# Output stage of a fused attention and gated-MLP kernel: order of the two products that share each PSUM bank

## The chip, the cores and the metric

The kernel runs on one core of one Trainium2 chip. The metric is device microseconds of one execution. Before the change it is 206.86 us, the median of 3 runs (206.8 to 207.03). Beside these there is one execution under the profiler, from which all rows below come.

## The reference

The input x has 2048 tokens of 512 features. It is normalised (xn), and three things are added: x itself, a local attention, and a gated MLP.

```python
xn = _layernorm(x)
# attention: 32 heads of 16; each token looks at 8 keys, 2 tokens apart, itself first
qkv = xn @ wqkv
o = softmax(q . k[s - 2*w]) . v[s - 2*w]      # w = 0..7, positions under 0 masked
A = o.reshape(S, 512) @ wo
# gated MLP: 688 + 688 features
z = gelu(xn @ w_in)
z1, z2 = z[:, :688], layernorm(z[:, 688:])
g = w_sp @ z2 + b_sp                          # 2048 x 2048, mixes tokens
B = (z1 * g) @ w_out
out = x + A + B
```

## The kernel before, in words

**Stages.** The first part (up to about 73 us) normalises x, makes z2, q, k and v, and forms the attention weights. The long middle part runs over 16 row tiles j of 128 tokens. `mix(j)` (line 488) multiplies the mixing matrix by z2 (32 matmuls, line 492), `z1_tile(j)` (line 500) makes the gate (8 matmuls, line 504), and `gate_out(j)` (line 512) multiplies the two on VectorE (line 514) and puts the product, transposed by a DMA, into `uT` (line 515). `uT` holds the gated features on partitions, in 6 chunks of 128, by 2048 tokens. Meanwhile VectorE forms the attention's outputs `op` in a generator `av_ops` (line 550), from which `vector_work(us)` (line 575) takes pieces; the last pieces are an addition at line 563, one at line 565 and the closing one at line 567, which writes `op` for the last quarter of the tokens. The order on every engine is the order in which the program issues: there is no scheduler.

**Layout of `op`.** Its 128 partitions are 4 bands of 32 heads; a band k holds 256 tokens of a half (half 0 is tokens 0 to 1023, half 1 the rest). On the free axis stand the 16 features of a head, and 512 columns: four blocks of 128 columns, which the program calls jj = 0 to 3. jj 0 and 1 belong to half 0, jj 2 and 3 to half 1. So a group jj is four token tiles, one for each band k, and the tile number is i = 8 (jj // 2) + 2 k + jj % 2.

**Output stage (lines 627 to 659).** A token tile's output is one PSUM bank, 128 tokens by 512 features in fp32, and is made of two products:

- the *attention's part* A(jj), line 635: 14 of the 16 head features (`DHA`), 56 matmuls for a group. Each uses 32 rows of the array (`tile_position=(32 * k, 0)`), and the four bands run beside each other into four banks. "A set" below is four such matmuls, one for each band.
- the *gated part* B(jj, k), line 646: 6 matmuls with all 128 rows for a token tile. The free rows of the last chunk of `uT` hold the two head features that A leaves out; `op_rest(hb, queue)` (line 543) copies them there by 8 DMAs for a half, for half 0 on SP's queue at j = 13, for half 1 on ScalarE's queue after group 0.

The eight banks are two pools of four, `ps_o[0]` for even jj and `ps_o[1]` for odd jj. The order on TensorE is A(0), A(1), B(0, 0..3), B(1, 0..3), then A(2), A(3), B(2, 0..3), B(3, 0..3). A opens a bank and B closes it. After each B(jj, k), VectorE adds the token tile of x (`xrs`, two buffers of four tiles, loaded by `load_xr`, line 585) to the bank and writes `ot` (line 650, four buffers), and SP stores `ot` (line 651). The bank of jj + 2 is the bank of jj, so A(2) waits for the evictions of group 0 and A(3) for those of group 1. The very last tile (3, 3) goes another way: its attention part is taken out early, with x added, into `rest` (line 654), and `last_tile` (line 614) makes B in two halves of 256 columns in banks of its own, with two shorter evictions (line 623) and two stores (line 624). `load_xr(2)` and `load_xr(3)` stand on SP's queue behind the stores of groups 0 and 1.

Of the kernel before, what the change touches and what calls it, by code (L numbers as in the profile page):

```python
# [7 lines left out]
BF16 = mybir.dt.bfloat16  # L8
F32 = mybir.dt.float32
ACT = mybir.ActivationFunctionType  # L10
ALU = mybir.AluOpType
PSUM = bass.MemoryType.PSUM

P = 128
S = 2048
D = 512
# [4 lines left out]
DHA = 14  # L21
# [5 lines left out]
NG = 4  # L27
# [4 lines left out]
MCH = 6  # L32
# [13 lines left out]
def kernel(  # L46
# [16 lines left out]
    V = nc.vector  # L63
    A = nc.scalar
    G = nc.gpsimd
    PE = nc.tensor
    SP = nc.sync

    x2 = A_x.rearrange("b s d -> (b s) d")
    out2 = out.rearrange("b s d -> (b s) d")  # L70
# [414 lines left out]
    uT = late.tile([P, MCH, S], BF16, name="uT")  # L485
# [48 lines left out]
    pwp = ctx.enter_context(tc.tile_pool(name="pwp", bufs=3, reuse_waits="tile", **right))  # L534
    xrp = ctx.enter_context(tc.tile_pool(name="xrp", bufs=2, reuse_waits="tile", **right))
    smp = ctx.enter_context(tc.tile_pool(name="smp", bufs=1, reuse_waits="tile", **right))
    otp = ctx.enter_context(tc.tile_pool(name="otp", bufs=4, reuse_waits="tile", **right))
    op = late2.tile([P, DH, NB * TG], BF16, name="op")
    wo_r = late2.tile([P, DHA, D], BF16, name="wo_r")
    wout = late2.tile([P, MCH, D], BF16, name="wout")  # L540
    G.memset(wout[32:64, MCH - 1, :], 0.0)

    def op_rest(hb, q):

        for k in range(NG):
            for e in range(2):
                q.dma_start(uT[64 + 32 * e:96 + 32 * e, MCH - 1, hb * SB + k * TG:hb * SB + (k + 1) * TG],
                             op[32 * k:32 * k + 32, DHA + e, hb * TG:(hb + 1) * TG])
# [26 lines left out]
    def vector_work(us):  # L575
        while us > 0:
            t = next(work, None)
            if t is None:
                return
            us -= t  # L580

    x_g = x2.rearrange("(b k q p) d -> b q p k d", b=NB, k=NG, q=2)
    xrs = []

    def load_xr(jj):
        xr = xrp.tile([P, NG, D], BF16, name="xr")
        SP.dma_start(xr[:], x_g[jj // 2, jj % 2])
        xrs.append(xr)

    vector_work(2.0)  # L590
    for j in range(3, NT):
        z1_tile(j, mix(j))
        if j == 3:
            pair_b.close()
            ps_o = [ctx.enter_context(tc.tile_pool(name="ps_o0", bufs=4, space=PSUM, reuse_waits="tile"))]
# [8 lines left out]
        if 6 <= j < 10:  # L604
            k = j - 6
# [8 lines left out]
    def last_tile(i, rest):  # L614

        ot = otp.tile([P, D], BF16, name="ot")
        for h in range(2):
            ns = slice(h * D // 2, (h + 1) * D // 2)
            po = ps_o[0].tile([P, D], F32, name="po")
            for m in range(MCH):  # L620
                PE.matmul(po[:, ns], uT[:, m, i * P:(i + 1) * P], wout[:, m, ns],  # L621
                          start=(m == 0), stop=(m == MCH - 1))
            V.tensor_tensor(ot[:, ns], po[:, ns], rest[:, ns], ALU.add)
            SP.dma_start(out2[i * P:(i + 1) * P, ns], ot[:, ns])


    ps_o.append(ctx.enter_context(tc.tile_pool(name="ps_o1", bufs=4, space=PSUM, side="right", reuse_waits="tile")))
    for pair in range(2):
        pos = {}
        for jj in (2 * pair, 2 * pair + 1):  # L630
            for k in range(NG):
                pos[jj, k] = ps_o[jj % 2].tile([P, D], F32, name="po")
            for d in range(DHA):
                for k in range(NG):
                    PE.matmul(pos[jj, k][:], op[32 * k:32 * k + 32, d, jj * P:(jj + 1) * P],  # L635
                              wo_r[32 * k:32 * k + 32, d, :],
                              start=(d == 0), stop=((jj, k, d) == (3, NG - 1, DHA - 1)), tile_position=(32 * k, 0))
        for jj in (2 * pair, 2 * pair + 1):
            hb, q = jj // 2, jj % 2
            for k in range(NG):  # L640
                i = 8 * hb + 2 * k + q
                if (jj, k) == (3, NG - 1):
                    last_tile(i, rest)
                    continue
                for m in range(MCH):
                    PE.matmul(pos[jj, k][:], uT[:, m, i * P:(i + 1) * P], wout[:, m, :],  # L646
                              start=False, stop=(m == MCH - 1))
                vector_work(2.0)
                ot = otp.tile([P, D], BF16, name="ot")
                V.tensor_tensor(ot[:], pos[jj, k][:], xrs[jj][:, k, :], ALU.add)  # L650
                SP.dma_start(out2[i * P:(i + 1) * P, :], ot[:])
                if (jj, k) == (2, 0):
                    rest = pwp.tile([P, D], F32, name="rest", tag="pw")
                    V.tensor_tensor(rest[:], pos[3, NG - 1][:], xrs[3][:, NG - 1, :], ALU.add)
            if jj == 0:
                vector_work(1e9)
                op_rest(1, A)
            if jj + 2 < 4:
                load_xr(jj + 2)


# [1 line left out]
_INS = ['A_x', 'A_wqkv', 'A_wo', 'B_x', 'B_w_in', 'B_w_sp', 'B_b_sp', 'B_w_out']  # L663
_OUTS = [((1, 2048, 512), 'bfloat16')]
# [25 lines left out]
```

## Time and profile before

| what | value |
|---|---|
| median of the runs | 206.86 us |
| the profiled execution, its own time | 206.6 us |
| its span, first to last instruction | 204.9 us |
| TensorE (PE) busy, share of the span | 200.3 us, 98% |
| VectorE (DVE) busy | 166.1 us, 81% |
| ScalarE (ACT) busy | 93.5 us, 46% |
| granted TensorE clock, mean | 0.999 |
| first matmul of the output stage | 168.64 us after the span's start |
| last eviction (line 623) begins | 202.01 us after the span's start |

How to read it: the page of a profile gives busy times, the span in 40 slices, the chain of work that ended last (followed back from the last instruction), and groups of instructions by source line. PE are matmuls and PEld the loads of the stationary operand, which overlap them. SPq and ACTq are the queues from which DMAs are issued. Matmuls are pipelined: one of 512 columns takes some 379 ns from start to end, while the next starts sooner, so a busy PE may still start its matmuls later than it could. Their ends are modelled and a few records are missing.

### The profile page before, as it was taken

The numbers are of one execution on the slowest core, as the hardware profiler recorded it, in microseconds if no ns is written. First come the engines' busy times: TensorE is split into PE (matmuls) and PEld (weight loads), VectorE is DVE, ScalarE is ACT, GpSimd is POOL, SyncE is SP. The second block draws the span as 40 slices with busy tenths as digits, with TensorE's granted clock in tenths as the row PEclk, the third lists the DMA queues.
The fourth block names the chain that finished last, engine by engine and source line by source line (L and its number), as shares of the span: only waits on it lengthen the run. The fifth ranks groups of instructions, "written<-read, shape, count | busy, mean of one in ns | idle before, by whom it ended". The sixth has DMA issues, their size and how long they took to land.

```text
span 204.9 us, 4056 instructions
## 1 busy us (share of the span) xinstructions
PE 200.3 (98%) x1660; PEld 120.7 (59%) x1666; DVE 166.1 (81%) x192; ACT 93.5 (46%) x145; POOL 16.1 (8%) x82
## 2 busy tenths in 40 slices
PE   7999999999999999999999999999999999999994
PEld 7755554555566666656666666666666664444442
DVE  4899949659299599989999999999999985582353
ACT  3868897676879996335733331213333320000000
POOL 5045630000000000100000000000000000000000
PEclk9999999999999999999999999999999999999999
DMA  6973846999000004718766799999565225047323
GB/s 170 363 223 78 198 95 154 213 212 117 4 3 0 3 0 44 154 32 163 122 129 141 179 210 187 218 175 187 114 145 140 56 48 80 26 99 218 110 99 97
DMA packets 67395, 25.64 MB, mean 125 GB/s; under 512 B 57152, under 2 KB 67248, under 8 KB 67248
## 3 DMA queue, kind: packets, MB, share of 16 engines
q1 hardware_dynamic: 66960, 25.24, 57.6%
q8 instruction: 13, 0.21, 0.4%
q10 hardware_dynamic: 416, 0.14, 0.3%
q14 instruction: 6, 0.05, 0.1%
HBM read 9.79 MB, written 2.10 MB: 58 GB/s over the span
## 4 chain that ended last, share of the span: by engine, by line
PE 96%; DVE 1%; DMA 1%; issue 0%
PE pg L492 36%; PE pq L260 10%; PE po L646 9%; PE pzb L229 9%; PE pz L504 9%; PE pv L285 7%; PE po L635 6%; PE pl L310 4%; PE pq L272 3%; DMA xq<-in_A_x_dram 1%; PE po L621 1%; PE pt L212 1%; DVE stats L185 1%; PE idle L100 0%; DVE xn L190 0%
## 5 line engine op out<-in xcount | busy, mean ns | idle before, releaser
L492 PE MATMUL pg<-z,wspT 128*128 128x344 bf16 x512 | 77.3, 309 | 0.0
L492 PEld LDWEIGHTS <-wspT 128*128 128x128 bf16 x512 | 50.0, 98 | 24.9 <-issue 0.4
L301 DVE TENSOR_TENSOR pr<-qk 128x8192 bf16<-128x8192 bf16 x8 | 35.0, 4420 | 7.4 <-PE pl L310 7.4
L495 ACT ACTIVATE gs<-pg,b_col 128x688 bf16<-128x688 f32 x16 | 13.3, 833 | 52.9 <-PE pg L492 52.9
L558 DVE TENSOR_TENSOR pw<-vp,a_sb 128x4096 bf16<-128x4096 bf16 x16 | 36.1, 2284 | 0.0
L650 DVE TENSOR_TENSOR ot<-po,xr 128x512 bf16<-128x512 f32 x15 | 10.2, 689 | 15.2 <-PE po L646 14.9
L260 PE MATMUL pq<-xnT,wqk 128*128 128x512 bf16 x93 | 21.4, 379 | 0.2
L504 PE MATMUL pz<-w_z,xnT 128*128 128x344 bf16 x128 | 21.3, 309 | 0.0
L229 PE MATMUL pzb<-w_z,xnT 128*128 128x344 bf16 x128 | 20.1, 309 | 0.0
L646 PE MATMUL po<-wout,uT 128*128 128x512 bf16 x88 | 19.3, 379 | 0.3 <-issue 0.3
L563 DVE TENSOR_TENSOR pw<-pw 128x4096 bf16<-128x4096 bf16 x8 | 18.3, 2288 | 0.1
L229 PEld LDWEIGHTS <-xnT 128*128 128x128 bf16 x128 | 12.3, 98 | 7.0 <-issue 0.4
L504 PEld LDWEIGHTS <-xnT 128*128 128x128 bf16 x128 | 12.4, 98 | 6.5 <-issue 0.4
L260 PEld LDWEIGHTS <-wqk 128*128 128x128 bf16 x96 | 9.3, 98 | 10.9 <-issue 0.4
L646 PEld LDWEIGHTS <-uT 128*128 128x128 bf16 x90 | 8.6, 98 | 11.0 <-issue 0.8
L263 ACT CAST qk<-pq 128x1024 bf16<-128x1024 f32 x12 | 12.1, 1012 | 5.4 <-PE pq L260 5.4
L285 PE MATMUL pv<-xnT,wv 128*32 128x512 bf16 x256 | 14.6, 380 | 0.0
L509 ACT ACTIVATE z<-pz 128x688 bf16<-128x688 f32 x16 | 11.9, 743 | 5.6 <-PE pz L504 5.2
L238 ACT ACTIVATE junk<-z 128x688 bf16<-128x688 bf16 x16 | 12.4, 778 | 0.2
L635 PE MATMUL po<-wo_r,op 32*128 32x512 bf16 x224 | 12.4, 375 | 0.0
L234 ACT ACTIVATE z<-pzb 128x688 bf16<-128x688 f32 x16 | 11.8, 735 | 1.4 <-PE pzb L229 1.4
L285 PEld LDWEIGHTS <-wv 128*32 128x32 bf16 x256 | 9.4, 139 | 4.6 <-issue 0.3
(81 smaller groups left out, 169.2 us busy)
## 6 DMA issues: line engine op xcount, KB each, us to landing
xr<-in_A_x_dram SPq DMA_DIRECT2D x4, 512.0 KB, 4.1
out_dram<-ot SPq DMA_DIRECT2D x15, 128.0 KB, 1.8
wo_r<-in_A_wo_dram SPq DMA_DIRECT2D x4, 448.0 KB, 4.8
w_z<-in_B_w_in_dram SPq DMA_DIRECT2D x2, 688.0 KB, 4.9
xq<-in_A_x_dram SPq DMA_DIRECT2D x2, 512.0 KB, 7.0
wqk<-in_A_wqkv_dram SPq DMA_DIRECT2D x2, 512.0 KB, 7.0
wout<-in_B_w_out_dram SPq DMA_DIRECT2D x1, 640.0 KB, 5.2
a_sb<-in_A_x_dram SPq DMA_DIRECT2D x1, 512.0 KB, 9.1
```

The costliest lines, as they stand in the source:

```text
L229: PE.matmul(pz[:, hh, 0:FHALF], xnT[:, kc, i * P:(i + 1) * P], w_z2[:, kc, hh * FHALF:(hh + 1) * FHALF], start=(kc == 0), stop=(kc == C - 1))
L238: A.activation(junk[:], z2[:, i, :], ACT.Square, accum_out=zsq[:, i:i + 1])
L260: PE.matmul(pq[:, s, :], wqk[:, kc, s, c * P:(c + 1) * P], xnT[:, kc, tsl], start=(kc == 0), stop=(kc == C - 1))
L285: PE.matmul(pv[32 * k:32 * k + 32, dd, :].rearrange("p (b t) -> p b t", b=NB), wv_v[:, kc, 2 * d2 + dd, :], xnT_g[:, kc, :, k, :], start=( ...
L301: V.tensor_tensor(pr[:], qk[hb][:, 0, :, HALO:HALO + SB].unsqueeze(1).broadcast_to([P, 2, C, SB]), shifted(qk[hb][:, 1, :, off:off + SB]), ...
L492: PE.matmul(pg[:, hh, 0:FHALF], wsps[j][:, k, :], z2[:, k, hh * FHALF:(hh + 1) * FHALF], start=(k == 0), stop=(k == NT - 1))
L495: A.activation(gs[:], pg[:, :, 0:FHALF], ACT.Identity, bias=b_col[:, j:j + 1])
L504: PE.matmul(pz[:, hh, 0:FHALF], xnT[:, kc, j * P:(j + 1) * P], w_z1[:, kc, hh * FHALF:(hh + 1) * FHALF], start=(kc == 0), stop=(kc == C - 1))
L558: V.tensor_tensor(pw[:], shifted(vp[:, :, hb, off:off + P]), a_sb[:, 2 * p:2 * p + 2, osl].unsqueeze(2).broadcast_to([P, 2, DH, P]), ALU.mult)
L563: V.tensor_tensor(pws[p - 1][:], pws[p - 1][:], pw[:], ALU.add)
L635: PE.matmul(pos[jj, k][:], op[32 * k:32 * k + 32, d, jj * P:(jj + 1) * P], wo_r[32 * k:32 * k + 32, d, :], start=(d == 0), stop=((jj, k, d ...
L646: PE.matmul(pos[jj, k][:], uT[:, m, i * P:(i + 1) * P], wout[:, m, :], start=False, stop=(m == MCH - 1))
```

## The change

The output stage is written in another order. The other functions, the data and the number of matmuls, evictions and DMAs are the same. On TensorE the order becomes B(0, 0..3), B(1, 0..3), which open all eight banks; then A(0), A(1), which close them; then A(2) and A(3), which open them anew; then B(2, 0..3), B(3, 0..3), which close them. The remaining attention work of VectorE and `op_rest(1, A)` are issued ahead of the first eviction. The four evictions and stores of group 0 follow A(0), those of group 1 follow A(1), with `load_xr(2)` and `load_xr(3)` behind them. `rest` is taken ahead of the eviction of (2, 0) and no longer behind it. In `last_tile` only the notation differs.

```diff
+    def out_b(jj, k, first):
+        i = tokens_of(jj, k)
+        if first:
+            pos[jj, k] = ps_o[jj % 2].tile([P, D], F32, name="po")
+        for m in range(MCH):
+            PE.matmul(pos[jj, k][:], uT[:, m, i * P:(i + 1) * P], wout[:, m, :],
+                      start=first and m == 0, stop=not first and m == MCH - 1)
...
+    def out_a(jj, first):
+        for k in range(NG):
+            if first:
+                pos[jj, k] = ps_o[jj % 2].tile([P, D], F32, name="po")
+        for d in range(DHA):
             for k in range(NG):
-                pos[jj, k] = ps_o[jj % 2].tile([P, D], F32, name="po")
-            for d in range(DHA):
-                for k in range(NG):
-                    PE.matmul(pos[jj, k][:], op[32 * k:32 * k + 32, d, jj * P:(jj + 1) * P],
-                              wo_r[32 * k:32 * k + 32, d, :],
-                              start=(d == 0), stop=((jj, k, d) == (3, NG - 1, DHA - 1)), tile_position=(32 * k, 0))
+                PE.matmul(pos[jj, k][:], op[32 * k:32 * k + 32, d, jj * P:(jj + 1) * P],
+                          wo_r[32 * k:32 * k + 32, d, :], start=first and d == 0,
+                          stop=(not first or (jj, k) == (3, NG - 1)) and d == DHA - 1, tile_position=(32 * k, 0))
...
+    for jj in range(2):
+        for k in range(NG):
+            out_b(jj, k, True)
+    vector_work(1e9)
+    op_rest(1, A)
+    for jj in range(4):
+        out_a(jj, jj > 1)
+        if jj < 2:
             for k in range(NG):
-                i = 8 * hb + 2 * k + q
...
-                vector_work(2.0)
-                ot = otp.tile([P, D], BF16, name="ot")
-                V.tensor_tensor(ot[:], pos[jj, k][:], xrs[jj][:, k, :], ALU.add)
-                SP.dma_start(out2[i * P:(i + 1) * P, :], ot[:])
-                if (jj, k) == (2, 0):
-                    rest = pwp.tile([P, D], F32, name="rest", tag="pw")
-                    V.tensor_tensor(rest[:], pos[3, NG - 1][:], xrs[3][:, NG - 1, :], ALU.add)
-            if jj == 0:
-                vector_work(1e9)
-                op_rest(1, A)
-            if jj + 2 < 4:
-                load_xr(jj + 2)
+                store(jj, k)
+            load_xr(jj + 2)
+    rest = pwp.tile([P, D], F32, name="rest", tag="pw")
+    V.tensor_tensor(rest[:], pos[3, NG - 1][:], xrs[3][:, NG - 1, :], ALU.add)
+    for jj in range(2, 4):
+        for k in range(NG):
+            if (jj, k) == (3, NG - 1):
+                last_tile(tokens_of(jj, k), rest)
+            else:
+                out_b(jj, k, False)
+                store(jj, k)
```

`store(jj, k)` is the eviction and the store of a tile as before (lines 649 to 651).

## The prediction

> **What bounds the kernel.** I read the page first, then the chain of waits in order of time, then the timeline of the output stage from 168 us on.
>
> From the page of before:
>
> ```profile
> PE 200.3 (98%) x1660; PEld 120.7 (59%) x1666; DVE 166.1 (81%) x192; ACT 93.5 (46%) x145; POOL 16.1 (8%) x82
> PEclk9999999999999999999999999999999999999999
> PE 96%; DVE 1%; DMA 1%; issue 0%
> L646 PE MATMUL po<-wout,uT 128*128 128x512 bf16 x88 | 19.3, 379 | 0.3 <-issue 0.3
> L646 PEld LDWEIGHTS <-uT 128*128 128x128 bf16 x90 | 8.6, 98 | 11.0 <-issue 0.8
> ```
>
> TensorE is the bound: 98% busy, 96% of the chain, at full clock all along. The last two lines show that two matmuls of line 646 have no record: 90 weight loads, 88 matmuls. That will matter.
>
> The end of the chain in order of time (start, length, engine, tile, line, count):
>
> ```profile
> 167.54 1.17 PE pz L504 x8
> 168.71 6.16 PE po L635 x112
> 174.87 0.16 issue
> 175.03 10.31 PE po L646 x47
> 185.33 6.15 PE po L635 x112
> 191.49 0.16 issue
> 191.65 9.01 PE po L646 x41
> ```
>
> Nothing but matmuls ends last in the output stage, and the only holes stand where the attention's part (L635) gives way to the gated part (L646). So only fewer holes or a new wait of TensorE can change the time.
>
> The timeline around a hole, and VectorE's part of the same time:
>
> ```profile
> 174.27 0.60 PE L635 MATMUL po<-wo_r,op 32*128 32x512 bf16 x8
> 174.80 0.55 PEld L646 LDWEIGHTS <-uT 128*128 128x128 bf16 x4 [0.42 <-issue]
> 175.03 0.59 PE L646 MATMUL po<-wout,uT 128*128 128x512 bf16 x2 [0.16 <-issue]
> ...
> 176.31 0.69 DVE L650 TENSOR_TENSOR ot<-po,xr 128x512 bf16<-128x512 f32 x1 [4.01 <-PE po L646]
> 176.91 2.28 DVE L565 TENSOR_TENSOR pw<-pw 128x4096 bf16<-128x4096 bf16 x1
> 179.11 0.69 DVE L650 TENSOR_TENSOR ot<-po,xr 128x512 bf16<-128x512 f32 x1
> 179.71 1.22 DVE L567 TENSOR_TENSOR op<-pw 128x2048 bf16<-128x2048 bf16 x1
> 180.85 1.88 DVE L650 TENSOR_TENSOR ot<-po,xr 128x512 bf16<-128x512 f32 x3
> ```
>
> **The step of a matmul.** 47 recorded matmuls take 10.31 us: (10.31 - 0.38) / 46 = 0.216 us from start to start. The attention's part has the same step for a set of four: the 28 sets of a pair of groups take 6.22 us in the timeline, (6.22 - 0.38) / 27 = 0.216.
>
> **What is removed: two changes of array mode.** TensorE changes between 128 rows and 32 rows four times now: gate to A(0), A(1) to B(0), B(1) to A(2), A(3) to B(2). After, the gate is followed by B (both 128 rows), so only B(1) to A(0) and A(3) to B(2) are left. The prices:
>
> - Gate to A: the gate's last matmul starts at 168.40, its step is 0.146 (1.17 / 8), the first of A is due at 168.55 and starts at 168.64: **0.09**.
> - A(1) to B and B to A(2) together: from the first matmul of A(0), 168.64, to that of A(2), 185.27, are 16.63 us. In them lie 28 sets and 48 matmuls, 76 x 0.216 = 16.42. The rest is **0.21** for the two.
> - A(3) to B: from 185.27 to the first matmul of line 621 at 200.50 are 15.23 us for 28 + 42 steps, 15.12: **0.11**.
>
> So each change costs about 0.10 us, 0.41 in all, of which 0.21 stay: **-0.20 us**. This is less than the rows seem to offer. The first B matmul is recorded at 175.03, 0.53 after the last set of A (174.49), which reads as a loss of 0.32; the weight loads sit idle 0.42. But this is where a record is missing: 48 loads stand against 47 matmuls in the stretch, the second load starts at 174.81, and elsewhere a load starts when the matmul ahead of it does. The eviction settles it. It begins at 176.31; other evictions begin 0.42 us after the sixth matmul of their tile starts (the one at 185.37 after the matmul of 184.96). Counted from an unrecorded matmul at 174.81 the sixth starts at 175.89, 0.42 before; counted from 175.03 it starts at 176.11, 0.20 before, which is shorter than the matmul's own 0.38.
>
> **What is moved, on TensorE.** B(0) and B(1) now start at 168.55. They need the gated features of tiles 0 to 7, whose transposes are long done, and the eight copies of half 0, the last of which SP issues at 164.20 and which land 1.8 later, at 166.0; the first use is later than 168.55. The banks of `ps_o[1]` are free when the last gate is evicted (168.80 + 0.74 = 169.54); B(1) gets there at 168.55 + 24 x 0.216 = 173.73. B ends at 168.55 + 48 x 0.216 = 178.92, so A(0) starts at 179.02, A(1) at 182.04, A(2) at 185.07, A(3) at 188.09, and B(2) at 179.02 + 56 x 0.216 + 0.10 = 191.22. Before, it starts at 191.65 - 0.22 = 191.43 (its first matmul is the other one without a record): again 0.21 earlier. From there on the order is the old one, with the same tail: last matmuls, evictions of 0.42, two stores.
>
> **What is moved, on VectorE.** Line 563 ends at 172.29, and lines 565 and 567 follow at once, as nothing of the stores stands between them: 172.3 + 2.2 + 1.2 = 175.8 in place of 180.9. A(2), which reads it, starts at 185.07. The 4.01 us for which VectorE now waits ahead of its first eviction cost nothing, and their going gains nothing. The eight copies of half 1 on ScalarE's queue start at 175.8 and take 5.1 us to issue, as now; the last landed 4.0 later at most, which would be 185, and B(2) asks for them after 191. The covers are 9 and 6 us.
>
> **The added wait: A(2) and A(3) on evictions just before them.** Now there are 6 to 8 us of B between the closing of a bank and its reuse. After, A(0) closes all four banks in its last set, and A(2) wants them one group later, 14 x 0.216 = 3.02 us. Behind a waiting matmul stands all of TensorE. A(0)'s last set starts at 179.02 + 13 x 0.216 = 181.83, the first eviction at +0.42 = 182.25; evictions follow each other at 0.60 (180.85, 181.45, 182.04: three in 1.88 us), and the fourth ends at 182.25 + 1.80 + 0.69 = 184.74, against 185.07: **0.33 us to spare**. Group 1: last set at 184.85, evictions from 185.27, the fourth ends at 187.76 against 188.09: again 0.33. An answer from VectorE to a waiting engine is quick: the store's issue stands at 177.03, 0.03 after the eviction's end at 177.00. So I take nothing for this wait; below nothing it cannot be.
>
> The rule that speaks against this is in the Trainium skill, "TensorEngine Tiling (Array Packing)", section "PSUM Bottleneck": after a fourfold faster TensorE the PSUM copy may become the bottleneck, and both ScalarE and VectorE should empty it. The row says 2.49 us of evictions against 3.02 us of matmuls, so here VectorE alone just holds. "TensorE: Matmul & The Clock Gate", section "The cost: per-tile semaphore tail", adds that the completions of packed tiles which each raise a semaphore are served one after another, 25 + 4.7 x 4 + 26.3 x 4 = 149 ns for four tiles, an estimate by its formula; no row of before has four such closings. It would eat less than half of the spare time and leave the sum as it is.
>
> **The buffers of the stores.** `ot` has four. The evictions of group 1 start 3.02 us after those of group 0 and need their stores landed. Store k is issued at 182.97 + 0.60 k, the eviction that reuses its buffer wants to start at 185.27 + 0.60 k: it waits where landing takes over 2.3 us. From the list of DMA issues, narrowed to the stores issued at 177.03, 179.83 and 183.53, and to the three from 197 to 201 (the last column is us to landing):
>
> ```profile
> out_dram<-ot SPq DMA_DIRECT2D x1, 128.0 KB, 1.7
> out_dram<-ot SPq DMA_DIRECT2D x1, 128.0 KB, 3.0
> out_dram<-ot SPq DMA_DIRECT2D x1, 128.0 KB, 3.7
> out_dram<-ot SPq DMA_DIRECT2D x3, 128.0 KB, 1.7
> ```
>
> The median of all 15 is 1.8. The one at 3.7, and another at 184.02 with the same time, were issued right behind the 512 KB load `xr` (182.58). After, the four stores of group 0 stand ahead of that load on SP and those of group 1 behind it, where nobody soon waits for them. So I take 1.8 and no wait, with 1.7 and 3.7 as ends.
>
> **The rest.** `load_xr(3)` is issued near 188.2 and lands 4.1 later, at 192.3. `rest` now stands ahead of (2, 0) on VectorE and waits for it until 192.3, so the eviction of (2, 0) starts near 192.9 and not at its 192.7; then 0.6 to 0.7 of VectorE face 1.30 of TensorE per tile, and this is caught up within a tile. Nothing. Evictions beside four-band matmuls: the one at 185.37 lies beside A(2) now, takes 0.69 as others do, and the sets beside it keep their step. Nothing.
>
> **Sum.** -0.20 us on an execution of 206.6 (204.9 of span and 1.7 around it) gives 206.4. The median of the runs is 0.26 above that execution, so I forecast **206.66**. About 0.2%, or 0.41 us, is what a measurement of this kernel can tell from no change; the gain is half of that.
>
> **Rivals.**
>
> 1. *The holes are as large as recorded.* Then a change from A to B costs 0.32, the one removed at the gate 0.09, and -0.41 or somewhat more follows: 206.4. For it stand the recorded starts, against it the missing record and the eviction at 176.31. 15%.
> 2. *A store lands late, by a little.* With landing time L the fourth eviction of group 1 ends at 184.77 + L + 0.69, and A(3) stalls for L - 2.63. At 3.0 (one store in the trace) the stall is 0.37, the net +0.17: 207.03, still no change to measure. 12%.
> 3. *VectorE's release of the banks becomes the bound (slower).* The same place, A(3) behind the evictions of group 1 behind the stores of group 0, at a landing of 3.7 as beside a 512 KB load: stall 1.07, net +0.87, 207.7. It decides for slower from L = 3.24 on. For it: those two stores; against it: their place behind the load, which these stores don't have. 12%.
>
> That the order isn't the one described is excluded: TensorE's instructions, listed, stand in it, and their number is the old one.
>
> **Chances and range.** Forecast 61% (2 of them spill over to faster and 1 to slower), rivals 15, 12 and 12. Faster by over 0.2%: 0.17. Within: 58 + 12 = 0.70. Slower: 0.13. The range takes in rivals 1 and 2 and the near end of 3: 206.35 to 207.3.
>
> **What would show it.** Right: L639 begins within 0.02 us of 168.55 with no hole, two holes are left, A(0) to A(3) run as 56 sets in 12.1 us, and VectorE's fourth evictions end 0.2 to 0.3 before A(2) and A(3). Wrong: an idle TensorE in front of A(2) or A(3) with an eviction (rival 3: behind a store) as releaser; or a span shorter by 0.4 or more with the same two holes (rival 1).

## The result, and the profile after

The changed kernel takes 207.8 us (median of 17 runs, 206.75 to 209.01), the kernel before in the same sessions 206.8 (17 runs, 206.47 to 207.91): ratio 1.0039, interval 1.0023 to 1.0055. It is slower by some 0.8 to 1.0 us, outside the range of the forecast, and its runs spread wider. The profiled execution took 207.98 us, its span is 206.3.

The first line of the page after hardly tells the difference: TensorE is at 98% as before, and VectorE a point lower.

```profile
PE 201.2 (98%) x1666; PEld 120.9 (59%) x1666; DVE 166.0 (80%) x192; ACT 93.6 (45%) x145; POOL 16.1 (8%) x82
```

The chain of waits in order of time (start, length, what) no longer consists of matmuls alone:

```profile
168.86 10.36 PE po L639 x48
179.22 3.17 PE po L648 x56
182.39 1.89 DVE ot L655 x3
...
184.29 3.30 DMA out_dram<-ot
...
188.33 1.29 DVE ot L655 x2
...
189.66 3.18 PE po L648 x53
192.84 9.17 PE po L639 x42
```

The first row answers to the forecast: the gated part follows the gate without a hole. Then the chain leaves TensorE for evictions of group 0 (L655), a store of theirs (`out_dram<-ot`, 3.30 us) and evictions of group 1, and comes back to TensorE only at 189.66, in A(3).

The timeline of the same stretch:

```profile
179.15 9.68 PE L648 MATMUL po<-wo_r,op 32*128 32x512 bf16 x170
182.38 2.48 DVE L655 TENSOR_TENSOR ot<-po,xr 128x512 bf16<-128x512 f32 x4 [6.35 <-PE po L648]
183.10 3.04 SPq L656 DMA_DIRECT2D out_dram<-ot  x4
...
187.12 2.48 DVE L655 TENSOR_TENSOR ot<-po,xr 128x512 bf16<-128x512 f32 x4 [2.26 <-DMA out_dram<-ot]
...
189.06 0.37 PE L648 MATMUL po<-wo_r,op 32*128 32x512 bf16 x1 [0.23 <-DVE ot L655]
189.66 3.18 PE L648 MATMUL po<-wo_r,op 32*128 32x512 bf16 x53 [0.23 <-DVE ot L655]
```

VectorE has done group 0 at 184.86. The first bank of group 1 is closed and could be emptied near 185.4, but VectorE starts at 187.12, after 2.26 us of idle time that a store ended. Its four evictions then free the banks one by one: the second, third and fourth matmul of A(3), each into a bank of its own, start 0.05 us after an eviction ends. A(3) is due at 179.15 + 42 x 0.216 = 188.22; its fourth matmul starts at 189.66. **Stall: 1.43 us.**

Why the stores are late, from the list of DMAs, each narrowed to a stretch of the trace (183.0 to 183.5, 183.5 to 184.2, 184.2 to 184.85, 184.85 to 186.1). An issue's last column is us to landing; a queue's are packets, MB and share of the 16 engines' time in the stretch:

```profile
out_dram<-ot SPq DMA_DIRECT2D x1, 128.0 KB, 3.8
out_dram<-ot SPq DMA_DIRECT2D x1, 128.0 KB, 3.6
q8 instruction: 1, 0.02, 13.4%
out_dram<-ot SPq DMA_DIRECT2D x1, 128.0 KB, 3.3
out_dram<-ot SPq DMA_DIRECT2D x1, 128.0 KB, 3.0
```

All four land late, and among them begins a transfer of another kind: one packet of 16 KB on an instruction queue. 13.4% of 16 engines over 0.65 us is 1.39 us on one engine. From 185.7 to 186.45 only 9 packets move in the whole core, one after the other, between two stretches at over 300 GB/s. Here is that stretch, and below it a store that had the DMA engines to itself, in the kernel before (177 to 179):

```profile
DMA packets 9, 0.01 MB, mean 11 GB/s; under 512 B 1, under 2 KB 9, under 8 KB 9
DMA packets 144, 0.13 MB, mean 66 GB/s; under 512 B 16, under 2 KB 144, under 8 KB 144
```

A whole store is 144 packets, 16 of them small; a sixteenth of it is 9 packets, one of them small. So the stretch is read as one engine of the sixteen working off its share of the first store, which had waited behind the fetch, while fifteen are done. The count fits, but that it is one engine stays inferred; the records do not name engines.

### The profile page after: what moved, and what is told of

It reads as the page before. It is cut to its first block, busy times and chain, and to the rows that moved or that the text cites. A ratio compares the mean times of both kernels' runs of the same rounds, so it can differ in the third digit from the quotient of the medians.

```text
span 206.3 us, 4066 instructions
## 1 busy us (share of the span) xinstructions
PE 201.2 (98%) x1666; PEld 120.9 (59%) x1666; DVE 166.0 (80%) x192; ACT 93.6 (45%) x145; POOL 16.1 (8%) x82
## 4 chain that ended last, share of the span: by engine, by line
PE 94%; DVE 2%; DMA 2%; ACT 1%; issue 0%; DVEq 0%
PE pg L492 36%; PE pq L260 10%; PE po L639 9%; PE pzb L229 9%; PE pz L504 9%; PE pv L285 7%; PE pl L310 4%; PE pq L272 3%; PE po L648 3%; PE idle L100 2%; DVE ot L655 2%; DMA out_dram<-ot 2%; PE po L621 1%; ACT xnT L214 1%; PE pt L212 0%
## 5 line engine op out<-in xcount | busy, mean ns | idle before, releaser
L639 PE MATMUL po<-wout,uT 128*128 128x512 bf16 x90 | 19.8, 379 | 0.0
L655 DVE TENSOR_TENSOR ot<-po,xr 128x512 bf16<-128x512 f32 x15 | 9.8, 686 | 11.9 <-PE po L648 6.4
L648 PE MATMUL po<-wo_r,op 32*128 32x512 bf16 x224 | 13.2, 374 | 0.5 <-DVE ot L655 0.5
```

## The experiments

**Theories.** F: the instruction fetch holds the stores of group 0 on one DMA engine, the four `ot` buffers pass the delay to VectorE's next evictions, these to the banks, and the banks to A(3). S: four stores in a row are slow by themselves. E: VectorE's evictions of four banks are too slow for one group of matmuls, whatever the stores do. The clean measure is the *stage*: from the start of the last gate matmul (line 504) to the start of the very last matmul (line 621) in the timeline, 33.29 us before and 34.50 after. The start of the kernel spreads by itself, as will be seen.

**e1: seven output buffers.**

```diff
-    otp = ctx.enter_context(tc.tile_pool(name="otp", bufs=4, reuse_waits="tile", **right))
+    otp = ctx.enter_context(tc.tile_pool(name="otp", bufs=7, reuse_waits="tile", **right))
```

> The changed kernel with seven output buffers ot instead of four, so that the evictions of (1,0), (1,1) and (1,2) no longer wait for a store of group 0 and (1,3) alone reuses the first buffer. Theory F (a 16 KB instruction fetch occupies one DMA engine while the four stores of group 0 pass, their landing takes 3.0 to 3.8 us, and the reuse of ot passes this on to VectorE, the banks and A(3)): the stores still land in 3 us or more, but VectorE starts on group 1 near 185.4 and A(3) loses at most 0.1; the median is 0.2 us under the kernel before, ratio 0.999, 1.2 us under the changed kernel. Theory S (four stores in a row are slow by themselves): the same time, it is told apart by the shift of the fetch. Theory E (the evictions of four banks are too slow for a group of 3.02 us, whatever the stores do): no change, 207.8.

Measured: median 206.88 us (11 runs), ratio 1.0000 (0.9991 to 1.0009). The timeline of its profile (the stage begins 0.83 us later here):

```profile
179.98 12.27 PE L648 MATMUL po<-wo_r,op 32*128 32x512 bf16 x224
183.21 2.48 DVE L655 TENSOR_TENSOR ot<-po,xr 128x512 bf16<-128x512 f32 x4 [6.35 <-PE po L648]
...
186.23 2.48 DVE L655 TENSOR_TENSOR ot<-po,xr 128x512 bf16<-128x512 f32 x4 [0.54 <-PE po L648]
```

All 56 sets run in one piece, and VectorE starts on group 1 exactly 3.02 us after group 0, though three of the four stores still land after 3.1, 2.8 and 2.5 us. The stage is 33.08. So theory E is out: evictions alone keep pace. The reuse of `ot` is what passes the delay on. The median was expected 0.2 us under the kernel before and did not show it; this was followed up in e6 and e9.

**e2 and e3: moving the fetch.** 104 more TensorE instructions at the very start, in the changed kernel (e2) and in the kernel before (e3):

```diff
-    spin(26)
+    spin(14)
+    for _ in range(64):
+        PE.matmul(idle[0:32, 0, 0:32], ones[:, 0:32], ones[:, 0:32], start=True, stop=True)
```

> The changed kernel with 52 more matmuls (104 more instructions with their weight loads) among the warm-up matmuls at the very start: 14 large and 64 small ones in place of 26 large ones. TensorE's instructions are fetched every 256, so the fetch at 184.4 should fall 104 instructions, that is 13 sets or 2.8 us, earlier in the output stage, near 181.6 after the same start, and end before the first store's packets. Theory F: the stores of group 0 land in about 1.8 us, no stall at A(3), the time is 0.2 us under the same edit of the kernel before (e3), and 1.2 under the changed kernel but for what the start costs. Theory S: the stores land in 3 us or more with no fetch among them and the time is 1 us over e3.

> The kernel before with the same edit at the start as e2, its control. Both theories: the time of the kernel before, within 0.3 us, plus or minus what the other warm-up does to the start; only the difference to e2 is used.

Measured: e2 206.40 us (11 runs), ratio to the kernel before 0.9987 (0.9977 to 0.9998); e3 206.77, ratio 1.0000 (0.9992 to 1.0009). In e2 the fetch begins 13.55 us after the last gate matmul, where it began 15.83 after in the changed kernel (2.3 us earlier; 2.8 had been expected), and is over before the first store's packets. The four stores of group 0 in e2, in their order:

```profile
out_dram<-ot SPq DMA_DIRECT2D x1, 128.0 KB, 1.8
out_dram<-ot SPq DMA_DIRECT2D x1, 128.0 KB, 1.7
out_dram<-ot SPq DMA_DIRECT2D x1, 128.0 KB, 1.7
out_dram<-ot SPq DMA_DIRECT2D x1, 128.0 KB, 1.8
```

Four stores in a row, 0.6 us apart, each on time: theory S is out. The stage is 33.08 in e2 and 33.29 in e3. The pair also explains the odd store that the prediction had seen, the one at 3.0 us in the kernel before, issued at 179.83. Its stretch of the trace (180.2 to 180.5) holds a fetch:

```profile
q8 instruction: 1, 0.02, 28.9%
```

In e3, where the fetches lie elsewhere, the same store is issued at 179.95 and lands after 1.7 us. In e7 below, again the kernel before with a fetch beside this store, it lands after 3.3.

**e4: eight changes of array mode.** The kernel before with each group's B right behind its A:

```diff
-    for pair in range(2):
-        pos = {}
-        for jj in (2 * pair, 2 * pair + 1):
...
-        for jj in (2 * pair, 2 * pair + 1):
-            hb, q = jj // 2, jj % 2
+    pos = {}
+    for jj in range(4):
+        for k in range(NG):
+            pos[jj, k] = ps_o[jj % 2].tile([P, D], F32, name="po")
...
+        hb, q = jj // 2, jj % 2
+        if jj == 3:
+            rest = pwp.tile([P, D], F32, name="rest", tag="pw")
+            V.tensor_tensor(rest[:], pos[3, NG - 1][:], xrs[3][:, NG - 1, :], ALU.add)
+        for k in range(NG):
```

> The kernel before with the order A(0) B(0) A(1) B(1) A(2) B(2) A(3) B(3): eight changes between 128 and 32 rows in place of four, and no bank that is reused soon after its closing. By the prediction's price of 0.10 us for a change: +0.41 us, ratio 1.002. By the price that the recorded starts suggest (0.32 from A to B, 0.09 from B to A): +0.83 us, ratio 1.004.

Measured: 207.21 us (12 runs), ratio 1.0026 (1.0012 to 1.004), +0.5 us with 0.25 to 0.8 inside the interval. The stage decides: 33.73 against 33.29, +0.43 for four more changes, **0.11 us each**. From its chain of waits:

```profile
168.85 3.13 PE po L634 x56
171.98 0.16 issue
172.14 5.13 PE po L647 x23
```

Again the first matmul behind each hole has no record (23 of 24), so each hole looks larger than it is. In the profile of e7 (the kernel before with another start, below) all 90 matmuls of this line are recorded, and a change can be read directly:

```profile
176.03 0.39 PE L637 MATMUL po<-wo_r,op 32*128 32x512 bf16 x4
176.35 0.39 PE L648 MATMUL po<-wout,uT 128*128 128x512 bf16 x1
```

From the start of the last set of A to that of the first matmul of B are 0.31 us there (the rows are rounded), a step of 0.216 and **0.09**; the change from B to A in the same profile gives 0.10. So the two readings, e4's stage and e7's records, put a change at 0.09 to 0.11.

**e5 and e7: the start of e2 without the shift.** 12 small matmuls in place of 64, so that TensorE has as many instructions as at first; in the changed kernel (e5) and the kernel before (e7):

```diff
-    for _ in range(64):
+    for _ in range(12):
```

> The start of e2 (14 large warm-up matmuls and small ones behind them), but 12 small ones in place of 64, so that TensorE has as many instructions as in the changed kernel and the fetch falls back to near 184.4, among the stores of group 0. Theory F: one or more of these stores land in about 3 us or more, A(3) loses 0.3 to 1.5, and the time is 0.5 to 1.3 us over its control e7. If the gain of e2 came from the other warm-up and not from the place of the fetch: the time is 0.2 to 0.4 us under e7.

> The kernel before with the start of e5, its control: the kernel before's time within 0.3 us, 33.29 us from the last gate matmul to the last matmul.

Measured: e5 208.92 us (6 runs), ratio 1.0108 (1.0083 to 1.0134); e7 208.16 (5 runs), ratio 1.0072 (1.006 to 1.0084). e7 missed its expectation: this shorter warm-up costs 1.4 us at the start, which both kernels share (in its profile the first 12 z2 matmuls take 3.11 us, 1.91 before, at a granted clock of 1.00; the cause was not looked for). Beside e7, e5 is 0.76 us slower, but its six runs spread from 208.19 to 210.13, so the profiles have to decide. In e5's profile the fetch is back at 16.19 us after the last gate matmul, the stores land after 3.9, 3.7, 3.4 and 3.1 us, and the stage is 34.59, against 33.29 in e7. So the gain of e2 came from the place of the fetch and not from the other warm-up.

**e6 and e8: seven buffers on both starts.** The edit of e1 in e5 (e6) and in e2 (e8).

> e5 with seven output buffers, to look again at what e1 left unclear (no stall in its profile, but a median of 206.88). Theory F: stores still late, no stall at A(3), last gate matmul to last matmul 33.08 us, time 0.2 us under e7. If seven buffers cost something of their own, or group 1 waits elsewhere in the unprofiled runs: the time is at e7 or above.

> e2 with seven output buffers: the version that should beat both kernels. Theory F: the stores of group 0 are on time already, so seven buffers change nothing: e2's 206.4, ratio 0.9985 to the kernel before. If seven buffers cost something of their own: over e2 by more than 0.1.

Measured: e6 207.82 us (12 runs), ratio 1.0045 (1.0024 to 1.0066), 0.34 under e7, with runs from 206.64 to 208.65, so that the medians alone do not show a gain; stores at 2.8 to 3.6 us, stage 33.08, 0.21 under e7's. e8 206.63 (11 runs), ratio 0.9994 (0.9983 to 1.0006); stores on time, stage 33.08. e8 missed e2's 206.40 by 0.23; its stage and what follows are the same, and in its profile the first matmul of q starts at 12.21 us, in e2's at 11.93.

**e9 to e12: more profiles of the same two kernels**, e1 (e9, e10) and the changed one (e11, e12).

> e1 once more, for its profile. If its median of 206.88 came from the start of the kernel: 33.08 us again from the last gate matmul to the last matmul, and the first matmul of q at another place than in the kernel before (11.94), up to 1 us later, by which the whole time differs. If seven buffers still leave a stall in some executions: over 33.1 from the last gate matmul to the last matmul.

> The same kernel as e9 in another execution: 33.08 us from the last gate matmul to the last matmul, and a start that differs, if the start is what spreads; over 33.1 if a stall is left in the output stage.

> The changed kernel once more, for its profile: how much of its spread of 2.3 us lies in the output stage. Theory F: the fetch begins 15.5 to 16.2 us after the last gate matmul, and the stage is 33.08 plus the stall that follows from the latest landing among the first stores of group 0; where only later stores are hit, the stall is smaller than 1.4.

> The same kernel as e11 in another execution: a fetch 15.5 to 16.2 us after the last gate matmul, late stores of group 0, and 33.08 us plus the stall that they make from the last gate matmul to the last matmul.

Measured, with the other profiles beside them:

| kernel | first q matmul | fetch after the last gate | landing of the stores of group 0 | stage | time of that execution |
|---|---|---|---|---|---|
| before | 11.94 | 11.89 | 1.7, 3.0, 1.9, 1.8 | 33.29 | 206.6 |
| changed | 12.09 | 15.83 | 3.8, 3.6, 3.3, 3.0 | 34.50 | 207.98 |
| changed (e11) | 12.32 | 15.70 | 4.1, 3.8, 3.5, 1.8 | 34.72 | 208.42 |
| changed (e12) | 12.11 | 15.98 | 1.8, 3.6, 3.3, 3.1 | 34.19 | 207.68 |
| seven buffers (e1) | 12.92 | 15.95 | 1.8, 3.1, 2.8, 2.5 | 33.08 | 207.38 |
| seven buffers (e9) | 12.05 | 15.70 | 3.8, 3.5, 3.2, 1.8 | 33.08 | 206.51 |
| seven buffers (e10) | 12.19 | 15.95 | 1.8, 3.5, 3.2, 3.0 | 33.08 | 206.65 |
| fetch moved (e2) | 11.93 | 13.55 | 1.8, 1.7, 1.7, 1.8 | 33.08 | 206.38 |

With seven buffers the stage is 33.08 in every profile; with four, and the fetch among the stores, it is 33.08 plus a stall of 1.1 to 1.6. The stall follows the first late store: where that is the first of the four (the changed kernel, e11 and e5), it is the landing time less 2.42 us each time. In e9 and e11 the fourth store was itself issued 1.2 and 1.5 us late, for a cause that was not looked for, so its 1.8 doesn't mean that it was done early. The rest of each execution's difference is the start: the load of z2's weights lands at a different time in each, the first q matmul comes some 5.15 us after it in all eight and the last gate matmul some 156.46 us after that, and 12.92 against 11.93 is a whole microsecond. This agrees with e1's flat median, but since only profiles show the start, that it makes the median of the unprofiled runs is not shown. In the session of e9 to e12 the kernel before ran once, without a profile, and took 207.93 us; so of these four the stages are compared with other sessions, and not the times. Nor is it shown what the fastest runs of the changed kernel (206.75) did; a fetch that misses the first stores would fit.

## Why the prediction was wrong, point by point

- **Two changes of mode go, -0.20 us: right.** The stage without a stall is 33.08 against 33.29, -0.22, and a change costs 0.09 (e7's records) to 0.11 (e4's stage) where the prediction had 0.10. Reading the missing record out of the count of weight loads and out of the eviction's start was right: where e7 has the record, the first B matmul starts 0.31 us after the last set of A and not 0.53. Rival 1, which took the holes as recorded, falls.
- **B first, `op` and the copies in time: right.** B starts 0.146 us after the last gate matmul, one ordinary step, and in e1 and e2 A(0) to A(3) run as 56 sets in one piece of 12.27 us, 55 steps of 0.216 and the length of the last matmul.
- **Evictions against a group, 0.33 us to spare: right.** In e2 they take 2.48 us of 3.02, and no matmul waits. The section "PSUM Bottleneck" of the page "TensorEngine Tiling (Array Packing)" in the Trainium skill was weighed rightly: by this case VectorE alone holds, as long as nothing holds VectorE.
- **The failed step is "So I take 1.8 and no wait, with 1.7 and 3.7 as ends".** The stores of group 0 landed after 3.8, 3.6, 3.3 and 3.0 us. The chain from there is the one of rival 3 (12%), and the sign it named, an idle TensorE before A(3) behind an eviction behind a store, is what the profile shows. It has the rival's place and nearly its price: with L = 3.8, the first store's, the prediction's L - 2.63 gives a stall of 1.2, measured 1.43; the sum had VectorE start at the landing, and it started 0.19 us after. But what made the stores late was not a 512 KB load, as the rival had it: they stand ahead of that load. It was the instruction fetch. This is the term that the prediction had put at nothing, and it outweighs the 0.2 us of gain.
- **Why it was missed.** The traces of before had the evidence. The page lists the instruction queue with 13 transfers and 0.21 MB, and one store in the very stage took 3.0 us where its neighbours took 1.8. The prediction used the median and kept the 3.0 as a rival's price, without asking what stood beside that store. A fetch stood there. The change then moved the densest stretch of TensorE instructions (8 for every 0.216 us in A, 2 in B) and with it the next fetch, right among the four stores that had just become urgent. The section "Instruction fetch mechanics" of the page "Runtime: NRT & Kernel Launch" in the Trainium skill says that instructions are refilled in blocks of 16 KiB, 256 instructions, by a DMA queue of the sequencer's own, at a cost mostly hidden. The traces agree on the blocks (13 of 16 KB for 3,332 matmuls and weight loads, one for 256 of them, and e2's 104 added instructions moved the fetch by 2.3 us). Hidden it is from TensorE, whose 56 sets ran in one piece beside a fetch in e1, but not from the stores.

The kernel before even shows the next link, in a row of its timeline that lies just behind the ones in the prediction:

```profile
182.95 0.69 DVE L650 TENSOR_TENSOR ot<-po,xr 128x512 bf16<-128x512 f32 x1 [0.22 <-DMA out_dram<-ot]
```

The store that took 3.0 us landed at 182.83 and held back the eviction that reuses its `ot` buffer, by 0.22 us. In the old order this cost TensorE nothing; its chain there holds nothing but matmuls and the two holes.

The version that is faster than both kernels is e2: 206.40 us, 0.9987 (0.9977 to 0.9998). Of its 0.37 us to its control e3, 0.22 is the stage, which is the gain that was forecast; in the two profiles the rest is the start (first q matmul at 11.93 and 12.07). That version depends on where the fetch falls. Seven buffers do not, and keep the stage at 33.08 in every profile, but on their own (e1, 206.88) their median isn't under the kernel before.

## What to carry to other kernels

A step that takes the slack out of a buffer's reuse turns a store's worst landing, not its median, into time: before counting on 1.8 us, look at each landing in the trace, and for every outlier at what else the DMA engines did then. In this kernel TensorE's instructions came by DMA, 13 times in each profile, about 256 instructions apart. Where a long unrolled stream issues many instructions in little time, look where its fetches fall, and give the transfers beside them a spare buffer. And a wider spread of the runs is a clue: here the changed kernel's stage took 34.19 to 34.72 us by how the fetch met the stores, where seven buffers gave 33.08 each time.

## What the runs showed of the hardware

One 16 KB instruction fetch took 0.88 to 1.71 us as a single packet in the output stages of these traces, and 128 KB stores that it caught landed after 2.5 to 4.1 us in place of 1.7 to 1.8. One store of the kernel before shows it alone: 3.0 and 3.3 us with a fetch beside it (before, e7), 1.7 without (e3). A change between 128 rows and 32 rows of the array costs 0.09 to 0.11 us, in either direction. And the start of this kernel spreads by up to 1 us from execution to execution of the same program (first matmul of q at 12.05 to 12.92 us in e1, e9 and e10).
